# Five of sixteen tiles of a normalised input transposed by DMA, with SyncE's queue in a written order, in a fused attention and SwiGLU gradient kernel

## The chip, the cores and the metric

The kernel runs on one core of a Trainium2 chip. Its engines are TensorE (PE: matmuls, with PEld for its weight loads), VectorE (DVE), ScalarE (ACT), GpSimd (POOL) and SyncE (SP), and 16 DMA engines move data. The metric is the device time of one execution in microseconds; lower is better. The kernel before was timed in three runs.

## The reference

x is 2048 x 640, 32 heads of 20. The kernel returns the block's output and, from grad_out, the gradients of x and of five weights.

```
phi = lambda t: jnp.where(t > 0, t + 1, jnp.exp(t)) + 1e-6
def A(x, wqkv, wo):                      # linear attention
    q, k, v = heads of x @ wqkv
    pq, pk = phi(q), phi(k)
    kv = jnp.einsum("bhsd,bhse->bhde", pk, v)
    z = jnp.einsum("bhsd->bhd", pk)
    num = jnp.einsum("bhqd,bhde->bhqe", pq, kv)
    den = jnp.einsum("bhqd,bhd->bhq", pq, z)[..., None] + 1e-6
    return (num / den) @ wo
def B(x, w_gate, w_up, w_down):          # SwiGLU
    return (silu(x @ w_gate) * (x @ w_up)) @ w_down
h = x + A(layernorm(x), wqkv, wo)
out = h + B(layernorm(h), w_gate, w_up, w_down)
out, vjp = jax.vjp(that, A_x, A_wqkv, A_wo, B_w_gate, B_w_up, B_w_down); grads = vjp(grad_out)
```

## The kernel before, in words

The 2048 rows are 16 tiles of 128 (ST = 16), and D = 640 is five blocks of 128 (DT = 5). The work goes stage by stage: first layer norm with k and q (the k/q stage), the products over all rows for attention (ps_y, ps_z, then small matrices), attention's output with the second layer norm (ps_a), the four groups of SwiGLU columns forward and backward (pg, pu, ps_dw), the gradients back through both layer norms (ps_dhn, ps_dp, ps_dk, ps_dxn), and at the end the output (ps_o) with dW_o and dW_v between its tiles. Small groups of matmuls that need only grad_out and w_down (ps_dm, line 405) are spread over the early stages.

The change touches the first of these. In the k/q stage each tile t passes through these steps, each on its own engine:

- `ln1_stats` (272 to 281): DVE takes mean and variance (lines 277 and 280). `ln_rstd` on GpSimd adds epsilon and raises to −0.5 (lines 139 and 140), which gives rstd1.
- `ln1_xn` (288): DVE writes the normalised tile xn from x, mean and rstd. The first three tiles are only centred, and are normalised again near the stage's end.
- `ln1_tr1` (302) and `copy1` (348): TensorE transposes xn in five matmuls against the identity into PSUM (ps_t), and ACT or DVE copies it to xnT. BY_V lists the tiles that DVE copies.
- `kq_mm` (311): 10 matmuls of 320 columns for k, then 10 for q, each followed on ACT by an exponential (316) and a Relu (317).
- `phi` (321 and 322): DVE joins two tiles of the exponential and the Relu into pk or pqa. After every fourth tile it issues the stores of pk, of pqa and of xnT to scratch in DRAM (326, 328 and 329), which later stages read back.

In iteration t of the loop TensorE runs k of tile t, the transposes of tile t + 1, and q of tile t. DVE runs the statistics of tile t + 3, phi of earlier tiles, and xn of tile t + 2 at the iteration's end. In this stage the orders of TensorE, DVE, ACT and GpSimd are the program's own (a manual schedule). SyncE's was left to the scheduler: after x and the k and q weights (wqk), `load_3` (line 218) puts the rest of x, wv and wo (wvo), wdT (three transposed pieces of w_down) and dh2T (grad_out, transposed by DMA in four parts of 512 rows), all in one row, and the stores stand behind. All these DMAs are issued by SP into one queue.

After the stage, `z_sum` (line 477) sums pk over all rows in matmuls with 32 columns of ones, four partial sums in four groups of 32 PSUM partitions. The sum has to be spread to all partitions in more than bf16's accuracy. Before, ACT and DVE each write one number per row with factors from `sgn`, so that half of the rows hold the rounded sum (high) and the others the remainder (low), and one pass of matmuls with `ones16` (2/H everywhere) adds them (ps_zb, 2 matmuls, at line 109 by the helper `mm_row`). GpSimd makes `hot` and `sgn` at the start (240 to 246). Late in the kernel `dwo` (947 to 953) makes one block of dW_o's rows by two matmuls, with all 128 columns of KV as weights.

Of the kernel before, what the change touches and what calls it, by code (L numbers as in the profile page):

```python
# [20 lines left out]
def kernel(  # L21
# [53 lines left out]
    def wk(name, w=D, pool=0):  # L75
        return wpools[pool].tile([P, w], BF16, name=name, tag="w", padded_shape=[P, D])
# [141 lines left out]
    def load_3():  # L218
        for t0 in range(4, ST, 2):
            yield load_x(nc.sync, t0, t0 + 2)  # L220
        yield nc.sync.dma_start(out=wvo[:, 0:5], in_=A_wqkv[:, 2 * D:3 * D].rearrange("(k p) n -> p k n", p=P))
        for j in range(HG):
            yield nc.sync.dma_start(out=wvo[:, 5 + j, :], in_=A_wo[OH[j]:OH[j] + P, :])
        yield load_wdT(wdT, 0)
        for c in range(4):
            yield nc.sync.dma_start_transpose(out=dh2T[:, :, c * 512:(c + 1) * 512], in_=go_flat[c * 512:(c + 1) * 512, :])
        yield load_wdT(wdT, 1)
        yield load_wdT(wdT3, 3)

    with tc.manual_schedule(engines={EngineType.Pool}):  # L230
        ident = const.tile([P, P], BF16, name="ident")
        make_identity(nc, ident[:])
        nhalf = const.tile([P, 4], FP32, name="nhalf")
        nc.vector.memset(nhalf[:], -0.5)
        ones = const.tile([P, P], BF16, name="ones")
        nc.vector.memset(ones[:], 1.0)
        E = const.tile([P, D], BF16, name="E")
        sgn = const.tile([P, 2], FP32, name="sgn")
        hot = const.tile([P, 8], FP32, name="hot")
        nc.gpsimd.memset(hot[:], 1.0)  # L240
        for sign in (1, -1):
            nc.gpsimd.affine_select(out=hot[:], in_=hot[:], pattern=[[-sign * 16, 8]], compare_op=ALU.is_ge, fill=0.0,
                                    base=0 if sign > 0 else 15, channel_multiplier=sign)
        nc.gpsimd.tensor_tensor(out=hot[:, 0:4], in0=hot[:, 0:4], in1=hot[:, 4:8], op=ALU.add)
        nc.gpsimd.tensor_tensor(out=sgn[:, 1:2], in0=hot[:, 1:2], in1=hot[:, 3:4], op=ALU.add)
        nc.gpsimd.tensor_scalar(out=sgn[:, 0:1], in0=sgn[:, 1:2], scalar1=-2.0, scalar2=1.0, op0=ALU.mult, op1=ALU.add)
    ones16 = const.tile([P, P], BF16, name="ones16")
    nc.vector.memset(ones16[:], 2.0 / H)
    zpad = const.tile([P, 4, 64], BF16, name="zpad")
    nc.vector.memset(zpad[:], 0.0)  # L250
    mask = const.tile([P, 160], BF16, name="mask")
# [8 lines left out]
    def load_wdT(dst, g):  # L260
        o = GM if g == 1 else 0
        return nc.sync.dma_start_transpose(out=dst[:, :, o:o + GW[g]], in_=B_w_down[GO[g]:GO[g] + GW[g], :])
# [6 lines left out]
    pk = big.tile([P, ST, D], BF16, name="pk", tag="B")  # L269
    pqa = big.tile([P, ST, D], BF16, name="pqa", tag="B")  # L270
    NC = 3
    BY_V = (1, 2, 3, 6, 9, 12)

    def ln1_stats(t):
        st6 = small.tile([P, 2, 6], FP32, name="st6", tag="st6")
        for ci, (n0, n1) in enumerate(NCH):
            st = nc.vector.bn_stats(out=st6[:, ci, :], in_=x_tm[t // 8][:, t % 8, n0:n1])
            if t == 0 and ci == 0:
                wait_for(st, load_2())
        nc.vector.bn_aggr(out=mv1[:, t, :], in_=st6[:].rearrange("p a b -> p (a b)"))  # L280
        ln_rstd(mv1[:, t:t + 1, :], rstd1, t, 1)
# [37 lines left out]
    def phi(which, t, n=2):  # L319
        e = (pk, pqa)[which][:, t:t + n, :]  # L320
        nc.vector.tensor_scalar(out=e, in0=e, scalar1=1.0, scalar2=1e-6, op0=ALU.min, op1=ALU.add)
        nc.vector.tensor_tensor(out=e, in0=e, in1=rr[:, 2 * which + t // 2 % 2, t % 2:t % 2 + n, :], op=ALU.add)
        if (t + n) % 4 == 0:
            sl = slice(t + n - 4, t + n)
            if which == 0:
                nc.sync.dma_start(out=scr_pk_v[:, sl, :], in_=pk[:, sl, :])
            else:
                nc.sync.dma_start(out=scr_pq_v[:, sl, :], in_=pqa[:, sl, :])
                nc.sync.dma_start(out=scr_xnT[sl].rearrange("t p k c -> p t k c"), in_=xnT[:, sl])

    PIECES = ((0, 3), (3, DT))

    with tc.manual_schedule(engines={EngineType.PE, EngineType.DVE, EngineType.Activation, EngineType.Pool}):

        ps = mm("ps_warm")

        def warm(n):
            for _ in range(n):
                nc.tensor.matmul(ps[:, 0, :P], lhsT=ident[:], rhs=ident[:], start=True, stop=True)

        def copies(t, eng_copy):
            for sl, src in ln1_tr(t):
                c = eng_copy(out=xnT[:, t, sl], in_=src)
                if t == 0 and sl.start == 0:
                    wait_for(c, load_3())

        def copy1(t):
            (nc.vector.tensor_copy if t in BY_V else nc.scalar.copy)(out=xnT[:, t], in_=ln1_tr1(t))

        warm(37)  # L350
        ln1_stats(0)
        ln1_centre(0, 0, 3 * P)
        ln1_centre(0, 3 * P, D)
        copies(0, nc.scalar.copy)
        warm(8)
        ln1_stats(1)
        ln1_centre(1)
        kq_mm(0, 0, lambda: copies(1, nc.vector.tensor_copy), PIECES)
        ln1_stats(2)
        ln1_centre(2)  # L360
        kq_mm(1, 0, None, PIECES)
        ln1_stats(3)
        kq_mm(0, 1, lambda: copy1(2), PIECES)
        phi(0, 0)
        ln1_xn(3)
        kq_mm(1, 1)
        for t in range(2, ST):
            if t == 2:
                ln1_stats(4)
            if t > 3 and t + 3 < ST:  # L370
                ln1_stats(t + 3)
            kq_mm(t, 0, (lambda: copy1(t + 1)) if t + 1 < ST else None)
            if t == 2:
                ln1_stats(5)
            if t == 3:
                ln1_stats(6)
            if t == ST - 1:
                phi(0, t - 1, 1)
            kq_mm(t, 1)
            if t == 3:  # L380
                phi(1, 0)
            elif t == ST - 1:
                phi(0, t, 1)
                phi(1, t - 3)
                phi(1, t - 1)
            elif t > 3:
                phi(t % 2, t - 2 - t % 2)
            if t + 2 < ST:
                ln1_xn(t + 2)
            if ST - NC - 1 <= t < ST - 1:  # L390
                ln1_xn(t - ST + NC + 1)

# [75 lines left out]
    with tc.manual_schedule(engines={EngineType.PE, EngineType.DVE, EngineType.SP}):  # L470
        yk = strips.tile([P, DT * D + HG * P], BF16, name="yk", tag="S")
        Yt = yk[:, :DT * D].rearrange("p (k n) -> p k n", k=DT)
        KVT = yk[:, DT * D:].rearrange("p (j c) -> p j c", j=HG)
        zs = wk("zs")
        zh = wk("zh")

        def z_sum():
            ps = mm("ps_z")
            for ci, (n0, n1) in enumerate(NCH):
                for t in range(ST):  # L480
                    q = t % 4 * H
                    nc.tensor.matmul(ps[q:q + H, ci, :320], lhsT=ones[:, :H], rhs=pk[:, t, n0:n1],
                                     start=(t < 4), stop=(t >= ST - 4))
            nc.scalar.activation(out=half(zh[:]), in_=row(ps), func=ACT.Copy, scale=sgn[:, 0:1])
            nc.vector.scalar_tensor_tensor(out=half(zs[:]), in0=row(ps), scalar=sgn[:, 1:2], in1=half(zh[:]),
                                           op0=ALU.mult, op1=ALU.add)
            nc.vector.memset(KVT, 0.0)

        for i in range(DT):
            ps = mm("ps_y")  # L490
            for ci, (n0, n1) in enumerate(NCH):
                for t in range(ST):
                    nc.tensor.matmul(ps[:, ci, :320], lhsT=xn[:, t, i * P:(i + 1) * P], rhs=pk[:, t, n0:n1],  # L493
                                     start=(t == 0), stop=(t == ST - 1))
                if (i, ci) == (0, 0):
                    z_sum()
            nc.scalar.copy(out=half(Yt[:, i, :]), in_=row(ps))
            if i == 0:
                ps_z = mm("ps_zb")
                mm_row(ps_z, lambda k: ones16[:], lambda k, n0, n1: zs[:, n0:n1], 1)  # L500
                nc.scalar.copy(out=half(zb[:]), in_=row(ps_z))
                masks()
            if 0 < i < 4:
                dm(1)
# [288 lines left out]
    with tc.manual_schedule(engines={EngineType.SP, EngineType.DVE}):  # L793
# [152 lines left out]
        def dwo(j):  # L946
            h0, h1 = HC[j]
            ev = wk("dwo", pool=j % 2)
            ps = mm("ps_dwo")
            for ci, (n0, n1) in enumerate(NCH):  # L950
                nc.tensor.matmul(ps[:, ci, :320], lhsT=KV[:, j, :], rhs=G[:, j, n0:n1], start=True, stop=True)
            nc.scalar.copy(out=half(ev[:]), in_=row(ps))
            nc.gpsimd.dma_start(out=out_3[OH[j] + h0:OH[j] + h1, :], in_=ev[h0:h1, :])

        def dwv(i):
            ev = wk("dwv", pool=1)
# [101 lines left out]
```

## Time and profile before

| | |
|---|---|
| median of 3 runs (lowest to highest) | 817.11 us (817.04 to 817.66) |
| the profiled execution | 817.11 us, of which the span from first to last instruction is 815.4 us |
| granted clock of TensorE | 1.00 |
| k/q matmuls | 320, from 6.5 us to 54.4 us |
| transposes of one tile at line 302 | 70 matmuls (14 tiles), from 10.4 us to 50.4 us |
| SP's queue over 0 to 70 us | 93.4% of the 16 DMA engines' time |
| DMAs out of the stage | 12 stores of 640 KB, issued from 39.7 to 58.0 us |

"Busy" is the time in which an engine has an instruction running. TensorE's matmuls overlap, so the distance from one's start to the next's is what a matmul costs, not its length. In a line of the timeline the first number is the start and the second the length of a run of like instructions, both in microseconds; then come engine, line, operation, tile written and tiles read, shape and count, and in brackets the idle time before it with what ended it. "SPq" is the sequencer that issues DMAs: its length is that of issuing. "Landing" is the time from the start of issue until all data has arrived.

### The profile page before, as it was taken

The page shows a single profiled execution, that of the slowest core. Times are in us where ns is not written, and L with a number is a line of the kernel's source. Part 1 is how long each engine was busy: PE and PEld are TensorE (multiplying, and loading weights), DVE is VectorE, ACT ScalarE, POOL GpSimd, SP SyncE. Part 2 cuts the span into 40 slices and gives each one's busy share as a digit, 9 for nine tenths or more (in the row PEclk, how much of TensorE's full clock was granted, in tenths as well). Part 3 has the DMA queues.
Part 4 walks back from the last instruction along what each step waited for, and adds up shares of the span by engine and source line. Part 5 has one row for each costly group of instructions (what it writes and reads, how often), then busy time and mean ns, then how long its engine had stood idle before and what let it go on. Part 6 is the DMA issues. An engine that isn't in the chain of part 4 may idle for free.

```text
span 815.4 us, 13981 instructions
## 1 busy us (share of the span) xinstructions
PE 810.0 (99%) x5538; PEld 520.2 (64%) x5538; DVE 442.6 (54%) x849; ACT 288.9 (35%) x406; POOL 193.1 (24%) x356
## 2 busy tenths in 40 slices
PE   8999999999999999999999999999999999999998
PEld 6776666555555555555566677777777777777676
DVE  7878787890086028800760147787892366631212
ACT  6982432660184026400831122322312133322010
POOL 4420022222512412221126401211220121112330
PEclk9999999999999999999999999999999999999999
DMA  9994789899769986994498747977499989999952
GB/s 302 193 360 88 171 185 291 184 254 190 201 142 205 224 196 150 213 231 116 117 255 178 276 94 221 217 202 175 113 241 176 170 157 182 169 200 254 250 158 79
DMA packets 278320, 158.61 MB, mean 195 GB/s; under 512 B 235052, under 2 KB 264877, under 8 KB 278256
## 3 DMA queue, kind: packets, MB, share of 16 engines
q1 hardware_dynamic: 251696, 82.12, 54.0%
q0 software_dynamic: 17744, 64.45, 25.5%
q10 hardware_dynamic: 8816, 11.16, 4.4%
q8 instruction: 43, 0.70, 0.4%
q14 instruction: 21, 0.17, 0.1%
HBM read 47.68 MB, written 53.66 MB: 124 GB/s over the span
## 4 chain that ended last, share of the span: by engine, by line
PE 97%; DMA 1%; DVE 1%; ACT 0%; issue 0%; SPq 0%; DVEq 0%; ACTq 0%
PE ps_dw L676 21%; PE ps_dhn L109 14%; PE ps_dxn L928 8%; PE ps_o L990 7%; PE pu L609 7%; PE pg L604 7%; PE ps_kq L311 5%; PE ps_dwqk L109 5%; PE ps_dm L405 5%; PE ps_y L493 3%; PE ps_dp L109 3%; PE ps_gt L735 3%; PE ps_dk L109 3%; PE ps_a L550 2%; PE pdm L405 2%; DMA xr<-in_A_x_dram 1%
## 5 line engine op out<-in xcount | busy, mean ns | idle before, releaser
L109 PE MATMUL ps_dhn<-wgT,cols 128*128 128x320 bf16 x864 | 119.5, 299 | 0.0
L676 PE MATMUL ps_dw<-dd,hn 128*128 128x448 bf16 (+1 forms) x640 | 118.8, 346 | 0.0
L109 PEld LDWEIGHTS <-cols 128*128 128x128 bf16 x864 | 84.4, 98 | 33.0
L676 PEld LDWEIGHTS <-hn 128*128 128x128 bf16 x640 | 62.5, 98 | 54.3
L678 DVE CAST dwev<-ps_dw 128x896 bf16<-128x896 f32 (+3 forms) x12 | 10.9, 908 | 127.3 <-PE ps_dw L676 109.6
L641 POOL DMA_DIRECT2D scr_dT<-stg x64 | 34.6, 541 | 166.6 <-DMA stg<-dd 165.6
L678 ACT CAST dwev<-ps_dw 128x896 bf16<-128x896 f32 (+1 forms) x20 | 17.6, 878 | 157.6 <-PE ps_dw L676 150.6
L147 DVE CUSTOM_DVE_ANT_0 lb_a<-lb_dy,hn 128x640 bf16<-128x640 bf16 x32 | 26.4, 825 | 76.0 <-ACT lb_dy L145 76.0
L609 PE MATMUL pu<-wgu,hnT 128*128 128x448 bf16 (+1 forms) x320 | 63.6, 346 | 0.0
L604 PE MATMUL pg<-wgu,hnT 128*128 128x448 bf16 (+1 forms) x320 | 63.6, 346 | 0.0
L990 PE MATMUL ps_o<-wd,mT 128*128 128x320 bf16 (+3 forms) x462 | 61.1, 295 | 0.0
L676 PE MATMUL ps_dw<-m_s,dh 128*128 128x448 bf16 (+1 forms) x320 | 60.4, 346 | 0.0
L928 PEld LDWEIGHTS <-ring 128*128 128x128 bf16 x480 | 46.9, 98 | 18.3
L990 PEld LDWEIGHTS <-mT 128*128 128x128 bf16 (+1 forms) x462 | 41.7, 97 | 17.5 <-issue 2.6
L928 PE MATMUL ps_dxn<-wqkvT,ring 128*128 128x320 bf16 x320 | 51.3, 299 | 0.0
L676 PEld LDWEIGHTS <-dh 128*128 128x128 bf16 x320 | 31.3, 98 | 27.1
L609 PEld LDWEIGHTS <-hnT 128*128 128x128 bf16 x320 | 31.3, 98 | 27.1
L604 PEld LDWEIGHTS <-hnT 128*128 128x128 bf16 x320 | 31.2, 98 | 27.1
L405 PE MATMUL ps_dm<-wdT,dh2T 128*128 128x448 bf16 (+1 forms) x240 | 47.0, 344 | 0.1
L405 PEld LDWEIGHTS <-dh2T 128*128 128x128 bf16 x320 | 31.0, 98 | 25.1 <-issue 0.3
L311 PE MATMUL ps_kq<-wqk,xnT 128*128 128x320 bf16 x320 | 46.3, 299 | 0.2
L145 ACT ACTIVATE lb_dy<-ps_dhn,rstd 128x640 bf16<-128x640 f32 x16 | 12.7, 793 | 88.6 <-PE ps_dhn L109 88.6
(171 smaller groups left out, 1274.7 us busy)
## 6 DMA issues: line engine op xcount, KB each, us to landing
scr_dT<-stg POOLq DMA_DIRECT2D x48, 224.0 KB, 3.6
cols<-scr_dT POOLq DMA_DIRECT2D x6, 1728.0 KB, 8.5
scr_m<-m_s POOLq DMA_DIRECT2D x12, 448.0 KB, 4.6
cols<-scr_dT ACTq DMA_DIRECT2D x2, 1728.0 KB, 8.8
out_dram<-dwev POOLq DMA_DIRECT2D x30, 112.0 KB, 3.3
scr_dT<-stg POOLq DMA_DIRECT2D x16, 192.0 KB, 2.4
scr_pk<-pk SPq DMA_DIRECT2D x4, 640.0 KB, 8.4
scr_xnT<-xnT SPq DMA_DIRECT2D x4, 640.0 KB, 8.5
```

The costliest lines, as they stand in the source:

```text
L109: nc.tensor.matmul(ps[:, ci, :320], lhsT=lhs(k), rhs=rhs(k, *NCH[ci]), start=(start and k == 0), stop=(stop and k == n - 1))
L147: nc.vector.tensor_tensor_reduce(out=a[:], in0=dy[:], in1=xhat, scale=1.0, scalar=0.0, op0=ALU.mult, op1=ALU.add, accum_out=sums[:, 1:2])
L311: nc.tensor.matmul(ps[:, ci, :320], lhsT=xnT[:, t, k, :], rhs=wqk[:, k, w0 + n0:w0 + n1], start=(k == 0), stop=(k == DT - 1))
L405: nc.tensor.matmul(ps[:, c, :w], lhsT=dh2T[:, kt, (t + c) * P:(t + c + 1) * P], rhs=wdT[:, kt, o:o + w], start=(kt == 0), stop=(kt == DT - 1))
L493: nc.tensor.matmul(ps[:, ci, :320], lhsT=xn[:, t, i * P:(i + 1) * P], rhs=pk[:, t, n0:n1], start=(t == 0), stop=(t == ST - 1))
L604: nc.tensor.matmul(pg[:, c, :w], lhsT=hnT[:, kt, (t + c) * P:(t + c + 1) * P], rhs=wg[:, kt, 0:w], start=(kt == 0), stop=(kt == DT - 1))
L609: nc.tensor.matmul(pu[:, c, :w], lhsT=hnT[:, kt, (t + c) * P:(t + c + 1) * P], rhs=wg[:, kt, w:2 * w], start=(kt == 0), stop=(kt == DT - 1))
L641: nc.gpsimd.dma_start(out=scr_dT[t + c, :, KO[g]:KO[g] + GK[g], :], in_=stg[:, :GK[g], :])
L676: nc.tensor.matmul(ps[:, c, :w], lhsT=lhs(t), rhs=rhs(t), start=(t == 0), stop=(t == ST - 1))
L678: last = copy(out=ev[:, :len(parts), :w], in_=ps[:, :len(parts), :w])
L928: nc.tensor.matmul(ps[:, ci, :320], lhsT=lhs[:, i, :], rhs=rhs[:, i, n0:n1], start=(k == 0 and i == 0), stop=(k == 2 and i == DT - 1))
L990: nc.tensor.matmul(po(t, ci), lhsT=mTs[t // 4][r, t % 4, j, :], rhs=wd[r, j, n0:n1], start=(t, ci) not in opened, stop=last)
```

## The change

The loads of dh2T's last two parts, of wv and of wo move out of `load_3` into functions of their own, and so do the stores out of `phi`. A table `after` says behind which iteration of the loop each is issued; SyncE joins the manual schedule, so that its DMAs stand in the program's order, and each waits there for its data. From tile XD = 11 on, xn is written one step earlier, at the start of iteration t for tile t + 2, and a DMA transpose issued right then writes xnT from it; TensorE's transposes and the PSUM copies of these five tiles go. Tile 12 leaves BY_V for that reason. The z broadcast uses two rounded parts in two tiles, high and low, hence four matmuls in place of two, and `hot` and `sgn` with their GpSimd instructions go. `dwo` computes only the 120 or 40 rows that are stored.

```
     def load_3():
         for t0 in range(4, ST, 2):
             yield load_x(nc.sync, t0, t0 + 2)
-        yield nc.sync.dma_start(out=wvo[:, 0:5], in_=A_wqkv[:, 2 * D:3 * D]...)
-        for j in range(HG):
-            yield nc.sync.dma_start(out=wvo[:, 5 + j, :], in_=A_wo[OH[j]:OH[j] + P, :])
         yield load_wdT(wdT, 0)
-        for c in range(4):
-            yield nc.sync.dma_start_transpose(out=dh2T[:, :, c * 512:(c + 1) * 512], in_=go_flat[c * 512:(c + 1) * 512, :])
-        yield load_wdT(wdT, 1)
-        yield load_wdT(wdT3, 3)
+        yield load_dh2T(0)
+        yield load_dh2T(1)
...
-    BY_V = (1, 2, 3, 6, 9, 12)
+    XD = 11
+    BY_V = (1, 2, 3, 6, 9)
...
+    after = {5: [(store_q, 0), (store_x, 0)], 6: [(load_dh2T, 2)], 7: [(load_dh2T, 3)], 8: [(load_wv,)], 9: [(store_q, 1)],
+             10: [(store_x, 1)], 11: [(load_wo, 0, 2)], 12: [(load_wo, 2, 4)], 13: [(load_wo, 4, 6), (store_q, 2), (store_x, 2)],
+             14: [(store_x, 3), (store_k, 0), (store_k, 1)],
+             15: [(store_k, 2), (load_wdT, wdT, 1), (store_q, 3), (store_k, 3), (load_wdT, wdT3, 3)]}
...
-    with tc.manual_schedule(engines={EngineType.PE, EngineType.DVE, EngineType.Activation, EngineType.Pool}):
+    with tc.manual_schedule(engines={EngineType.PE, EngineType.DVE, EngineType.Activation, EngineType.Pool, EngineType.SP}):
...
         for t in range(2, ST):
             if t == 2:
                 ln1_stats(4)
+            if XD <= t + 2 < ST:
+                ln1_xn(t + 2)
+                nc.sync.dma_start_transpose(out=xnT[:, t + 2], in_=xn[:, t + 2, :])
             if t > 3 and t + 3 < ST:
                 ln1_stats(t + 3)
-            kq_mm(t, 0, (lambda: copy1(t + 1)) if t + 1 < ST else None)
+            kq_mm(t, 0, (lambda: copy1(t + 1)) if t + 1 < XD else None)
...
-            if t + 2 < ST:
+            if t + 2 < XD:
                 ln1_xn(t + 2)
             if ST - NC - 1 <= t < ST - 1:
                 ln1_xn(t - ST + NC + 1)
+            for f, *a in after.get(t, ()):
+                f(*a)
...
-            nc.scalar.activation(out=half(zh[:]), in_=row(ps), func=ACT.Copy, scale=sgn[:, 0:1])
-            nc.vector.scalar_tensor_tensor(out=half(zs[:]), in0=row(ps), scalar=sgn[:, 1:2], in1=half(zh[:]),
-                                           op0=ALU.mult, op1=ALU.add)
+            nc.scalar.copy(out=half(zs[0][:]), in_=row(ps))
+            nc.vector.tensor_tensor(out=half(zs[1][:]), in0=row(ps), in1=half(zs[0][:]), op=ALU.subtract)
...
-                mm_row(ps_z, lambda k: ones16[:], lambda k, n0, n1: zs[:, n0:n1], 1)
+                mm_row(ps_z, lambda k: ones32[:], lambda k, n0, n1: zs[k][:, n0:n1], 2)
...
-                nc.tensor.matmul(ps[:, ci, :320], lhsT=KV[:, j, :], rhs=G[:, j, n0:n1], start=True, stop=True)
-            nc.scalar.copy(out=half(ev[:]), in_=row(ps))
-            nc.gpsimd.dma_start(out=out_3[OH[j] + h0:OH[j] + h1, :], in_=ev[h0:h1, :])
+                nc.tensor.matmul(ps[:h1 - h0, ci, :320], lhsT=KV[:, j, h0:h1], rhs=G[:, j, n0:n1], start=True, stop=True)
+            nc.scalar.copy(out=half(ev[:h1 - h0, :]), in_=ps[:h1 - h0, :, :320])
+            nc.gpsimd.dma_start(out=out_3[OH[j] + h0:OH[j] + h1, :], in_=ev[:h1 - h0, :])
```

More of the change, by code (lines that the diff above doesn't have):

```diff
@@ L220, in load_3, with load_dh2T, load_wv, load_wo @@
             yield load_x(nc.sync, t0, t0 + 2)
-        yield nc.sync.dma_start(out=wvo[:, 0:5], in_=A_wqkv[:, 2 * D:3 * D].rearrange("(k p) n -> p k n", p=P))
-        for j in range(HG):
-            yield nc.sync.dma_start(out=wvo[:, 5 + j, :], in_=A_wo[OH[j]:OH[j] + P, :])
         yield load_wdT(wdT, 0)
-        for c in range(4):
-            yield nc.sync.dma_start_transpose(out=dh2T[:, :, c * 512:(c + 1) * 512], in_=go_flat[c * 512:(c + 1) * 512, :])
-        yield load_wdT(wdT, 1)
-        yield load_wdT(wdT3, 3)
+        yield load_dh2T(0)
+        yield load_dh2T(1)
+    def load_dh2T(c):
+        return nc.sync.dma_start_transpose(out=dh2T[:, :, c * 512:(c + 1) * 512], in_=go_flat[c * 512:(c + 1) * 512, :])
+    def load_wv():
+        nc.sync.dma_start(out=wvo[:, 0:5], in_=A_wqkv[:, 2 * D:3 * D].rearrange("(k p) n -> p k n", p=P))
+    def load_wo(j0, j1):
+        for j in range(j0, j1):
+            nc.sync.dma_start(out=wvo[:, 5 + j, :], in_=A_wo[OH[j]:OH[j] + P, :])
     with tc.manual_schedule(engines={EngineType.Pool}):
@@ L237 @@
         E = const.tile([P, D], BF16, name="E")
[L238 to L248, printed above, removed]
+    ones32 = const.tile([P, P], BF16, name="ones32")
+    nc.vector.memset(ones32[:], 1.0 / H)
     zpad = const.tile([P, 4, 64], BF16, name="zpad")
@@ L322, in phi, with store_k, store_q, store_x @@
         nc.vector.tensor_tensor(out=e, in0=e, in1=rr[:, 2 * which + t // 2 % 2, t % 2:t % 2 + n, :], op=ALU.add)
[L323 to L329, printed above, removed]
+    def store_k(c):
+        nc.sync.dma_start(out=scr_pk_v[:, 4 * c:4 * c + 4, :], in_=pk[:, 4 * c:4 * c + 4, :])
+    def store_q(c):
+        nc.sync.dma_start(out=scr_pq_v[:, 4 * c:4 * c + 4, :], in_=pqa[:, 4 * c:4 * c + 4, :])
+    def store_x(c):
+        nc.sync.dma_start(out=scr_xnT[4 * c:4 * c + 4].rearrange("t p k c -> p t k c"), in_=xnT[:, 4 * c:4 * c + 4])
+    after = {5: [(store_q, 0), (store_x, 0)], 6: [(load_dh2T, 2)], 7: [(load_dh2T, 3)], 8: [(load_wv,)], 9: [(store_q, 1)],
+             10: [(store_x, 1)], 11: [(load_wo, 0, 2)], 12: [(load_wo, 2, 4)], 13: [(load_wo, 4, 6), (store_q, 2), (store_x, 2)],
+             14: [(store_x, 3), (store_k, 0), (store_k, 1)],
+             15: [(store_k, 2), (load_wdT, wdT, 1), (store_q, 3), (store_k, 3), (load_wdT, wdT3, 3)]}
     PIECES = ((0, 3), (3, DT))
-    with tc.manual_schedule(engines={EngineType.PE, EngineType.DVE, EngineType.Activation, EngineType.Pool}):
+    with tc.manual_schedule(engines={EngineType.PE, EngineType.DVE, EngineType.Activation, EngineType.Pool, EngineType.SP}):
         ps = mm("ps_warm")
@@ L473 @@
         KVT = yk[:, DT * D:].rearrange("p (j c) -> p j c", j=HG)
-        zs = wk("zs")
-        zh = wk("zh")
+        zs = [wk("zs"), wk("zl")]
         def z_sum():
```

## The prediction, as it was put on record

> **What bounds the kernel.** I read four views, from the whole to the place of the change. The page's first and fourth parts:
>
> ```profile
> PE 810.0 (99%) x5538; PEld 520.2 (64%) x5538; DVE 442.6 (54%) x849; ACT 288.9 (35%) x406; POOL 193.1 (24%) x356
> ...
> PE 97%; DMA 1%; DVE 1%; ACT 0%; issue 0%; SPq 0%; DVEq 0%; ACTq 0%
> ```
>
> TensorE is busy 99% of the span, and the chain that ended last is 97% TensorE. So an edit is worth the TensorE time that it takes away, less any wait that it brings. The stretches of the k/q stage (11.5 to 52 us) and of what follows it show whether that holds there (busy PE, PEld, DVE, ACT, POOL; granted clock; DMA share; GB/s):
>
> ```profile
> 11.50:35.00 23.50, 23.50 (x194) 17.46 (x194) 20.84 (x50) 22.68 (x36) 9.76 (x17) 1.00 1.11 249
> 35.00:52.00 17.00, 17.00 (x145) 12.71 (x143) 14.73 (x34) 16.25 (x28) 7.48 (x13) 1.00 1.09 311
> 52.00:62.00 10.00, 10.00 (x98) 6.93 (x97) 5.64 (x11) 6.17 (x10) 0.00 (x0) 1.00 1.04 355
> 62.00:97.00 35.00, 35.00 (x270) 22.68 (x269) 26.88 (x20) 12.99 (x17) 0.00 (x0) 1.00 0.61 125
> ```
>
> TensorE is never idle here and its clock is full, but the DMA share is 1.0 or more until 62 us: the queue into which the new transposes go is full. DVE is 87 to 89% busy. The timeline of one iteration, and the z broadcast:
>
> ```profile
> 41.15 0.44 PE L302 MATMUL ps_t<-ident,xn 128*128 128x128 bf16 x5
> 41.43 2.88 PE L311 MATMUL ps_kq<-wqk,xnT 128*128 128x320 bf16 x20
> ...
> 60.14 0.44 PE L109 MATMUL ps_zb<-zs,ones 128*128 128x320 bf16 x2
> 60.41 4.51 PE L493 MATMUL ps_y<-pk,xn 128*128 128x320 bf16 x32
> ```
>
> Starts are what count, since matmuls overlap: five transposes hold TensorE from 41.15 to 41.43, 0.28 us, and the two z matmuls from 60.14 to 60.41, 0.27 us. In the chain of waits 30 k/q matmuls take 4.08 us, so 20 take 2.72; with 0.28 that is the 3.0 us period of an iteration. The queue and DVE:
>
> ```profile
> 24.65 0.82 DVE L322 TENSOR_TENSOR pqa<-pqa,rr 128x1280 bf16<-128x1280 bf16 x1
> ...
> 34.40 0.44 DVE L288 TENSOR_SCALAR xn<-x_tm,mv,rstd 128x640 bf16<-128x640 bf16 x1
> 34.76 0.88 DVE L277 BATCH_NORM_STATS2 st<-x_tm 128x6 f32<-128x320 bf16 x2
> ...
> 35.67 0.21 DVE L280 BATCH_NORM_AGGREGATE mv<-st 128x2 f32<-128x12 f32 x1
> ...
> 36.40 1.19 POOL L140 TENSOR_TENSOR rstd<-lnv,nhalf 128x1 f32<-128x1 f32 x1
> ```
>
> The first row is when q's tiles 2 and 3 are finished, for which SP will wait; the others are DVE's and GpSimd's steps from xn(10) to the rstd of tile 12, whose lengths set how early an xn can go to the queue.
>
> **What goes, and what comes (TensorE).** The transposes of tiles 11 to 15 (at 38.15, 41.15, 44.14, 47.14 and 50.13) go: 5 x 0.28 = −1.40 us. The z broadcast has four matmuls for two: +0.27. Its inputs take as long as before: a plain ACT copy (a 128x640 PSUM cast took 0.70) for a scaled one (0.79), and a DVE subtraction (a 128x640 operation with PSUM took 0.82) for the three-operand one (0.88). In before the second ended at 59.79, 0.2 us ahead of the weight load at 60.01; without that cover a late input would cost its lateness. Net −1.13.
>
> **Edits at nothing.** The GpSimd setup that goes lies at 1.3 to 8.6 us, and TensorE waits there for DVE's xn (5.49). The four ACT copies and the DVE copy (0.69 and 0.49 each) go from engines that TensorE does not wait for. The dW_o matmuls keep 320 moving columns, hence their time. wv and wo are needed from 85 us and land by about 55; wdT's later parts from about 94. DMA drained by about 65 in before; the added transposes (4 us) and a gap of some 3 us move that to about 72, and the pqsT transposes, issued at 70, are first read at 97.6: their cover is 10 us.
>
> **The new wait.** k/q of tile t now waits for a DMA. Without the transposes, TensorE would reach tile 11 at 39.5 (38.15 + 10 matmuls), and then 42.2, 44.95, 47.7 and 50.4. Two chains feed it.
>
> First, DVE and GpSimd. xn(11) now follows xn(10) directly: 34.8 to 35.2. Then each xn needs its rstd: statistics 1.1 us, then GpSimd, whose power at 36.40 lasted 1.19 because it ended 0.4 after DVE's two-operand operation at 36.34 (elsewhere it took 0.57). Per tile: xn 0.4, statistics 1.1, phi 1.3, 0.4 of waiting: 3.2 us against TensorE's 2.72. So xn is ready at 35.2, 38.4, 41.6, 44.9 and 48.1. The pqsT transposes, the same size out of SBUF, landed 2.7 us after issue (median), 1.2 of it issue: 37.9, 41.1, 44.3, 47.6, 50.8. By this chain alone only tile 15 is late, by 0.4.
>
> Second, the queue itself. Landings stood in order of issue and a fixed distance apart: dh2T at 27.8, 31.7, 34.5, 37.7 (3.3 apart, from 2.8 to 3.9), the 640 KB stores from 44.1 to 65.2 (1.9 apart), wv 2.3 behind the last load of x (19.2 after 16.9). SP now holds back the first stores until phi of q's tiles 2 and 3 (25.5, the row at 24.65). Stores of 800 KB into an emptier queue landed 4.4 after issue, so this one of 640 KB at about 29.4. Behind it in order: xnT store 31.3, dh2T 2 at 34.6, dh2T 3 at 37.9, wv 40.2, and xnT of tile 11 (a quarter of a dh2T, 0.8) at 41.0: 1.5 late. With the shortest distances (1.7, 2.8, 2.8, 2.0, 0.7) it is 39.4, on time; with the longest (3.1, 3.9, 3.9, 2.7, 0.9) 43.9, 4.4 late. The next two each have one store ahead (1.9 + 0.8 = 2.7, TensorE's own pace), the last two only 320 KB: once late, the queue brings no further loss. Behind each waiting transpose on SP stand only stores and weights that nobody needs before 64 us.
>
> So the stall is 0.4 (DVE's chain) to 4.4 us. I take 1.0, between the DVE chain's 0.4 and the mean queue's 1.5, because dh2T's spacing of 3.3 is also SP's own time to issue one (3.1), and two smaller transposes at the end of the row (wdT, 448 and 384 rows) landed 2.8 and 1.9 apart, 3.2 and 2.5 per 512 rows: the DMA engines alone may be quicker than the mean.
>
> [...] The trace has SBUF transposes of five 128x128 blocks landing in 2.7 us. [...] Here 640 KB of dh2T took 3.3 us where a store of 640 KB took 1.9. [...]
>
> **Sum.** The profiled execution took 817.11 us, of which 815.4 span; it equals the median of the runs shown. 817.11 − 1.40 + 0.27 + 1.0 = 817.0.
>
> **Rivals.**
> - Forecast (0.42): the first DMA transpose arrives about 1 us late (0.6 to 1.6 of stall), and most of the saving is given back: 816.6 to 817.6.
> - On time (0.30): the queue is quicker than its mean; the stall is 0 to 0.6, and the time 817.11 − 1.13 to + 0.6 = 816.0 to 816.6. For it: the shortest distances. Against it: DMA share above 1.0.
> - Late queue (0.25): the place is SP's queue between 25.5 us and tile 11; two stores, two dh2T and wv stand ahead of the first transpose. Its price is the lateness of tile 11 with what the following tiles add; it makes the kernel slower from a stall of 1.13, and measurably (0.2%, 1.6 us) from 2.8. At the longest distances it gives 817.11 − 1.13 + 4.4 = 820.4.
> - The change does more than it says (0.03): DVE and ACT, relieved of copies, let TensorE gain elsewhere; nothing supports it, since TensorE has no idle time to win in the stage. Below 815.5.
>
> About 0.2% (1.63 us) is what a measurement of this kernel can tell from no change. Even on time the gain is 1.13, so faster gets the last rival and a share of error in my sums, 0.04. Slower needs a stall over 2.8: 0.14, of the late queue's 0.25. Same 0.82. The range runs from on time, 815.9, to a stall of 3, 819.0.
>
> **What would show it.** In the profile after: ps_t x45 instead of x70 at the one-tile line; a wait of TensorE (or its weight load) at tile 11's k/q, near 39.5 us, released by the DMA into xnT, of about 1 us, and small ones at 12 to 15; the first xnT transpose landing near 40.5. ps_zb x4 with 0.55 us. The z sum at 56.75 in before would begin near 56.4. If xnT 11 lands before 39.5, the second rival holds; if tiles 12 and 13 stall too, my claim that the queue keeps pace is wrong. I am wrong altogether if another place shows a TensorE wait, at ps_dm (64 us, for dh2T) or ps_a (97 us, for pqsT).

## The result, and the profile after

| | before | after |
|---|---|---|
| median (lowest to highest, 6 runs each) | 817.08 us (816.69 to 817.66) | 819.77 us (818.77 to 820.23) |
| ratio, 95% interval | | 1.0031 (1.0018 to 1.0044) |
| the profiled execution, its span | 817.11 us, 815.4 us | 820.23 us, 818.3 us |
| granted clock over the span | 1.00 | 0.997 |

The change costs 2.7 us, a little more than the range allowed (819.0). The six runs of after fall into two groups, which the explanation needs: three have a mean clock of 1.000 (818.77, 818.99, 819.53) and three one of 0.997 or 0.998 (820.01, 820.14, 820.23). The profile is one of the second group.

The page of after, its first part and the chain that ended last:

```profile
PE 811.3 (99%) x5515; PEld 521.0 (64%) x5515; DVE 442.2 (54%) x848; ACT 287.3 (35%) x402; POOL 193.3 (24%) x350
...
PE 97%; DMA 2%; DVE 1%; SPq 0%; issue 0%; DVEq 0%
```

TensorE has 23 instructions fewer (25 transposes less, two z matmuls more) and is busy 1.3 us longer: busy time rose while work fell, so some of the work ran slower. DMA's share of the chain went from 1 to 2%. The stretches of the stage (columns as before: busy PE, PEld, DVE, ACT, POOL; granted clock; DMA share; GB/s) show where:

```profile
11.50:35.00 23.50, 23.50 (x195) 17.47 (x194) 20.82 (x50) 22.63 (x36) 10.19 (x17) 1.00 0.98 220
35.00:52.00 17.00, 14.71 (x100) 9.92 (x99) 13.34 (x30) 12.31 (x20) 8.32 (x13) 0.90 1.05 258
```

The second row is the one that changed in kind. Between 35 and 52 us TensorE is idle for 2.29 us, and the clock granted in that stretch is 0.90. The timeline of TensorE from there:

```profile
42.01 15.43 PE L308 MATMUL ps_kq<-wqk,xnT 128*128 128x320 bf16 x100 [2.29 <-DMA xnT<-xn]
57.28 2.34 PE L500 MATMUL ps_y<-pk,xn 128*128 128x320 bf16 x16
...
62.93 0.30 PE L109 MATMUL ps_zb<-zs,ones 128*128 128x320 bf16 x1
...
63.34 0.30 PE L109 MATMUL ps_zb<-zl,ones 128*128 128x320 bf16 x1
63.48 0.71 PE L500 MATMUL ps_y<-pk,xn 128*128 128x320 bf16 x4
```

The 100 matmuls are tiles 11 to 15, and one wait stands ahead of them. By starts, the last matmul of tile 10 is at 39.42 and the first of tile 11 at 42.01; less one matmul's 0.14 that is a stall of 2.45 us. No later tile waits. But tile 11 took 4.40 us (42.01 to 46.41), and tiles 12 to 15 took 2.72 each. The small stretches around it give the reason:

```profile
39.00:42.00 3.00, 0.72 (x6) 0.29 (x3) 2.40 (x6) 2.16 (x4) 1.54 (x2) 1.00 1.12 328
42.00:43.00 1.00, 0.99 (x6) 0.65 (x7) 0.97 (x4) 0.00 (x0) 0.17 (x1) 0.72 1.04 382
43.00:44.00 1.00, 1.00 (x5) 0.55 (x4) 0.90 (x2) 0.00 (x0) 0.92 (x2) 0.50 1.20 341
...
45.00:46.00 1.00, 1.00 (x6) 0.55 (x4) 0.97 (x4) 0.81 (x2) 0.00 (x0) 0.57 1.24 282
46.00:47.00 1.00, 1.00 (x10) 0.73 (x8) 0.90 (x2) 0.39 (x1) 0.86 (x2) 1.00 0.75 211
```

After the idle time the clock falls to 0.5, at 42.444, and stays there for 3.413 us; TensorE is "busy" all along, with 5 matmuls in a microsecond where it has 10 afterwards. That costs 3.413 / 2 = 1.7 us and is no idle time at all, so a list of waits doesn't show it. Why tile 11 was late, SP's queue tells:

```profile
25.55 0.38 SPq L325 DMA_DIRECT2D scr_pq<-pqa  x1
25.98 0.65 SPq L328 DMA_DIRECT2D scr_xnT<-xnT  x1
26.67 9.09 SPq L226 DMA_TRANSPOSE dh2T<-in_grad_out_dram  x2
35.80 0.58 SPq L229 DMA_DIRECT2D wvo<-in_A_wqkv_dram  x1
36.48 1.21 SPq L376 DMA_TRANSPOSE xnT<-xn  x1
```

Two dh2T transposes took SP 9.09 us to issue behind the two stores: the first 5.8, where one took 3.1 to 3.6 in before. So SP reached tile 11's transpose at 36.48, while DVE had written that tile at 35.25. It landed at 41.97, 5.5 after its issue, behind dh2T's last part (37.8) and wv (41.42). The answers on the single issues give the microseconds from issue to landing, in order from 25.55 on (read with the starts above; the second dh2T was issued at 32.50):

```profile
scr_pq<-pqa SPq DMA_DIRECT2D x1, 640.0 KB, 5.0
scr_xnT<-xnT SPq DMA_DIRECT2D x1, 640.0 KB, 6.1
dh2T<-in_grad_out_dram SPq DMA_TRANSPOSE x1, 8.6
dh2T<-in_grad_out_dram SPq DMA_TRANSPOSE x1, 5.3
wvo<-in_A_wqkv_dram SPq DMA_DIRECT2D x1, 800.0 KB, 5.6
xnT<-xn SPq DMA_TRANSPOSE x1, 5.5
```

So tile 11 landed 0.55 us behind wv, and wv 3.6 behind dh2T's last part.

**The account of the profiled execution.** Transposes −1.38, z broadcast +0.27, stall +2.45, half clock +1.7: +3.0, against +2.9 of span (818.3 − 815.4). Up to the first ps_y matmul (54.49 before, 57.28 after) it is +2.8, pg stands 2.76 later (146.02, 148.78) and the last matmul 2.98 (812.09, 815.07): nearly all of it happens in the stage.

### The profile page after: what moved, and what is told of

Same layout as the page of the kernel before. It is cut to its first block, busy times and chain, and to the rows that moved or that the text cites. A ratio compares the mean times of both kernels' runs of the same rounds, so it can differ in the third digit from the quotient of the medians.

```text
span 818.3 us, 13931 instructions
## 1 busy us (share of the span) xinstructions
PE 811.3 (99%) x5515; PEld 521.0 (64%) x5515; DVE 442.2 (54%) x848; ACT 287.3 (35%) x402; POOL 193.3 (24%) x350
## 4 chain that ended last, share of the span: by engine, by line
PE 97%; DMA 2%; DVE 1%; SPq 0%; issue 0%; DVEq 0%
PE ps_dw L683 21%; PE ps_dhn L109 14%; PE ps_dxn L935 8%; PE ps_o L997 7%; PE pg L611 7%; PE pu L616 7%; PE ps_dwqk L109 5%; PE ps_dm L414 5%; PE ps_kq L308 4%; PE ps_y L500 3%; PE ps_gt L742 3%; PE ps_a L557 3%; PE ps_dk L109 3%; PE ps_dp L109 3%; PE pdm L414 2%; DMA xnT<-xn 1%
## 5 line engine op out<-in xcount | busy, mean ns | idle before, releaser
L648 POOL DMA_DIRECT2D scr_dT<-stg x64 | 34.6, 541 | 160.2 <-DMA stg<-dd 160.0
L616 PEld LDWEIGHTS <-hnT 128*128 128x128 bf16 x320 | 31.3, 98 | 27.1
L683 PEld LDWEIGHTS <-dh 128*128 128x128 bf16 x320 | 31.3, 98 | 27.1
L611 PEld LDWEIGHTS <-hnT 128*128 128x128 bf16 x320 | 31.3, 98 | 27.0
```

The costliest lines, as they stand in the source:

```text
L611: nc.tensor.matmul(pg[:, c, :w], lhsT=hnT[:, kt, (t + c) * P:(t + c + 1) * P], rhs=wg[:, kt, 0:w], start=(kt == 0), stop=(kt == DT - 1))
L616: nc.tensor.matmul(pu[:, c, :w], lhsT=hnT[:, kt, (t + c) * P:(t + c + 1) * P], rhs=wg[:, kt, w:2 * w], start=(kt == 0), stop=(kt == DT - 1))
L648: nc.gpsimd.dma_start(out=scr_dT[t + c, :, KO[g]:KO[g] + GK[g], :], in_=stg[:, :GK[g], :])
L683: nc.tensor.matmul(ps[:, c, :w], lhsT=lhs(t), rhs=rhs(t), start=(t == 0), stop=(t == ST - 1))
```

## The experiments

Theory at the start: the late queue, one wait at tile 11 from what SP has ahead of the first transpose, and the half clock that follows from the idle time. Rivals: that SP's written order, or the z broadcast and the small edits, cost time by themselves; that DVE's chain is too slow for transposes by DMA in any order. "Control" is the kernel before, timed beside each experiment.

### e1: wv behind the first transposes

```
-  8: [(load_wv,)], 11: [(load_wo, 0, 2)], 12: [(load_wo, 2, 4)]
+  11: [(load_wv,)], 12: [(load_wo, 0, 4)]
```

> The changed kernel with wv's load moved from iteration 8 to iteration 11 of the loop and wo's first part from 11 to 12, so that 800 KB less stands ahead of the transposes of tiles 11 and 12. If the wait at tile 11 comes from what is queued ahead of its transpose (theory), wv's 2.0 us between two landings (39.4 to 41.4 in the changed kernel) go, tile 11 lands near 40.0 in place of 42.0, TensorE waits 0.4 us in place of 2.5 and keeps its clock: about 817.1, 2.0 under the changed kernel's undisturbed runs and 3.0 under those that lost the clock. If it comes from xn's own lateness or from the transposes' own latency (rival), the landing stays near 42 and the time near 819.8.

Measured: 818.40 us (817.47 to 821.65, 12 runs), control 816.99, ratio 1.0024 (1.0013 to 1.0035); the theory had said 817.1. Its 39.4 for dh2T's last part in the changed kernel is a misreading, the median of two issues taken for one: that part landed at 37.8, so wv's share was 3.6 us and not 2.0. Without wv ahead of it tile 11 landed at 38.9, 2.6 after its issue (36.23) and 0.6 behind dh2T's last part, and didn't wait: the stall of after was wv's place. But TensorE's timeline has two new waits, at tile 13 (the row names ACT, but that tile's transpose landed at 46.22) and at tile 14, and SP's rows show what stood ahead of the second:

```profile
46.27 2.89 PE L308 MATMUL ps_kq<-wqk,xnT 128*128 128x320 bf16 x20 [0.77 <-ACT pqa L313]
51.44 7.28 PE L308 MATMUL ps_kq<-wqk,xnT 128*128 128x320 bf16 x40 [2.28 <-DMA xnT<-xn]
```

```profile
43.35 0.58 SPq L229 DMA_DIRECT2D wvo<-in_A_wqkv_dram  x1
45.30 1.20 SPq L376 DMA_TRANSPOSE xnT<-xn  x1
```

Tile 14's transpose (45.30) is now behind wv, which landed at 50.70, and the stall of 2.45 us has moved from tile 11 to tile 14, with a half clock again (0.5 from 51.465 for 3.413 us). Tile 15's (48.76), behind four loads of wo, came in time. The load was relocated, not removed. Four of the twelve runs are at 820.38 to 821.65 and the others at 817.47 to 818.74. Of the four, one has a mean clock of 0.998, one of 0.999 (which single runs of the control have too) and two of 1.000, so the half clock alone doesn't explain that group.

### e2: nothing ahead of the transposes that can wait

```
     def load_3(): ...
-        yield load_dh2T(0); yield load_dh2T(1)
+        for c in range(4): yield load_dh2T(c)
+        yield load_wv()
-    after = {5: [(store_q, 0), (store_x, 0)], 6: [(load_dh2T, 2)], 7: [(load_dh2T, 3)], 8: [(load_wv,)], ...
+    after = {9: [(store_q, 0)], 10: [(store_x, 0)], 11: [(store_q, 1)], 12: [(store_x, 1)], 13: [(load_wo, 0, 4)], ...
```

> The changed kernel with all four parts of dh2T and wv issued right behind x, before the loop, and one 640 KB store behind each of the transposes of tiles 11 to 14 (the stores wait longer). Theory: the queue is empty when tile 11 is issued at 35.3; it lands 2.7 to 3.0 us later, before 39.5; the later ones are held by the DVE and GpSimd chain (xn ready every 3.2 us), which makes tile 15 late by 0.4 us or so: 817.1 - 1.38 + 0.27 + 0.4 = 816.4. Rival (a DMA transpose with stores beside it always takes over 5 us): stall near 1 to 2 us again, 817.5 or more.

Measured: 816.88 us (816.48 to 818.19, 11 runs), control 816.99, ratio 0.9999 (0.9990 to 1.0007). All runs have a clock of 1.000. (The theory had said 816.4.) With the same transposes and the same matmuls, and only other places for them in SP's queue, the whole loss is gone: the late queue is shown. SP's rows for the first three transposes, and TensorE:

```profile
35.13 1.20 SPq L376 DMA_TRANSPOSE xnT<-xn  x1
...
38.37 1.20 SPq L376 DMA_TRANSPOSE xnT<-xn  x1
...
41.60 1.29 SPq L376 DMA_TRANSPOSE xnT<-xn  x1
```

```profile
45.61 8.49 PE L309 MATMUL ps_kq<-wqk,xnT 128*128 128x320 bf16 x60 [0.58 <-DMA xnT<-xn]
53.93 2.34 PE L500 MATMUL ps_y<-pk,xn 128*128 128x320 bf16 x16
```

SP now waits for DVE: the issues are 3.23 us apart, the pace of DVE's and GpSimd's chain. One stall is left, at tile 13 (0.75 us, its transpose landed at 45.56, 4.0 after issue), and 0.16 at tile 14. ps_y begins at 53.93, 0.56 earlier than in before.

### e3 and e4: the order alone, the z broadcast alone

e3 is after with `XD = 16` and tile 12 back in BY_V: all transposes are TensorE's, the rest is the change. e4 is before with only the two z parts (`zs`, `zl`, `ones32`, four matmuls).

> The changed kernel with all tiles transposed on TensorE as before (XD = 16, tile 12 copied by DVE again) but SP's queue in its written order and the four z matmuls. Theory: the loss is all in the DMA transposes of the five tiles, so that only the z broadcast's 0.27 us remains: 817.4. Rival (the written order of SP, with the later weights behind the stores, costs by itself somewhere after the stage): 818 or more.

> The kernel before with the change's z broadcast alone (four matmuls over high and low parts; the GpSimd setup of the sign columns goes), all else as before. Theory: two more matmuls on the path, +0.27 us, 817.3. Rival (the shorter setup and the simpler ACT and DVE steps pay for it, or the extra wait for the low part costs more): 817.0 or less, or over 817.6.

Measured: e3 817.50 us (817.06 to 818.82, 11 runs), control 816.99, ratio 1.0004 (0.9996 to 1.0013); e4 817.56 us (817.02 to 823.44, 11 runs), control 817.11, ratio 1.0010 (0.9996 to 1.0024). Neither interval excludes no change. Against their controls they are +0.51 and +0.45, 0.06 us apart. e3 has the written order of SP's queue and the smaller `dwo` beyond what e4 has, so those edits cost nothing that can be seen; the intervals reach some 0.7 and 1.1 us to either side. What the two share is the z broadcast, for which 0.27 was expected.

### e5 and e8: the stall without idle time

Ahead of tile 11's k in the kernel after, 16 (e5) or 8 (e8) matmuls that nothing reads, into a PSUM tile of their own:

```
+            if t == XD:
+                pf = mm("ps_fill")
+                for _ in range(16):
+                    nc.tensor.matmul(pf[:, 0, :320], lhsT=ident[:], rhs=wqk[:, 0, 0:320], start=True, stop=True)
```

> The changed kernel with 16 matmuls of 320 columns (some 2.2 us), whose result nobody reads, put on TensorE where it waits for tile 11. They lie inside the wait, so by themselves they cost next to nothing. Theory (two terms: a wait of 2.5 us, and a window of 3.41 us at half clock behind it in some of the runs, 1.7 us): the clock stays at 1.000 in every run and the median comes to that of the changed kernel's runs without the loss, 818.9, with no run above 819.6. Rival (the half clock isn't set by that wait, or the spread of the changed kernel's runs has another source): the runs still lie in two groups, 818.9 and 820.1, some at 0.997.

> The changed kernel with 8 unread matmuls (1.1 us) in TensorE's wait for tile 11 in place of 16, which leaves about 1.4 us of it idle. Theory (what loses the clock is the length of the idle time, 2.5 us with none, none lost with 0.3 left): with 1.4 us idle the clock holds too, 818.9 in all runs. Rival (any idle of over a microsecond can lose it): some runs near 820.1 at a clock of 0.997 again.

Measured: e5 818.99 us (818.74 to 820.41, 9 runs), control 816.99, ratio 1.0025 (1.0016 to 1.0035); e8 819.41 us (818.90 to 820.11, 9 runs), control 817.11, ratio 1.0027 (1.0017 to 1.0037). The stretch of e5, then of e8:

```profile
35.00:52.00 17.00, 16.79 (x127) 11.76 (x125) 14.45 (x32) 13.61 (x23) 8.33 (x13) 1.00 1.06 256
```

```profile
35.00:52.00 17.00, 15.46 (x117) 10.77 (x115) 14.47 (x33) 13.43 (x22) 8.33 (x13) 1.00 1.07 257
```

Tile 11 starts as late as in after (41.94 and 42.26), but the clock stays 1.00. None of the 18 runs has a clock below 0.999, where three of after's six had 0.997 or 0.998. So the half clock in this place comes from TensorE's idle time: 2.45 us of it was enough in half of six runs, about 1.4 us (e8) in none of nine. (A low clock isn't confined to this wait: one run of e4, whose profile has no such wait, took 823.44 us at 0.996.) It is also seen what it is worth: e5's median equals that of after's three undisturbed runs, 818.99, and the other three lie 1.15 us higher (820.14). The larger part of the loss, some 2 us, remains without it: it is the stall, less what the transposes save. e8 lies 0.5 over its forecast of 818.9 although its clock held; in its profile tile 11 starts 0.3 later than in e5, and tile 13 waits 0.5 where it waits 0.25 in e5.

### e6 and e7: the best order with before's z, and DVE's statistics taken ahead

e6 is e2 with the z broadcast of before. e7 is e6 with the statistics of tiles 12 to 15 taken an iteration or more earlier, and xn of tile 10 ahead of phi, so that SP gets its tiles sooner:

```
-            if t > 3 and t + 3 < ST:
-                ln1_stats(t + 3)
+            if t > 3 and t + 3 + (t >= 9) < ST:
+                ln1_stats(t + 3 + (t >= 9))
...
+                if t == 8:
+                    ln1_xn(10)
...
+            if t == 7:
+                ln1_stats(12)
```

> The kernel with dh2T and wv early and the stores behind (the second experiment, 816.88) with the z broadcast of before. Theory: that experiment's time less the two matmuls, 0.27 us: 816.6, 0.4 under before, of the saving of 1.38 some 1.0 lost to waits at tiles 13 to 15, whose xn comes every 3.2 us. Rival (the z edit costs nothing): 816.9.

> The kernel e6_best with the statistics of tile 12 taken in iteration 7, from then on one tile further ahead, and xn of tile 10 ahead of phi in iteration 8, so that no xn waits for GpSimd's rstd. Theory (the remaining waits come from the chain statistics, GpSimd's power, xn): xn comes every 2.8 us in place of 3.2, tile 15 is ready at 46.4 in place of 48.1, no wait is left, and the whole saving of 1.38 us shows: 815.7. Rival (the waits that are left are the queue's, from the store ahead of each transpose): 816.6, as e6_best.

Measured: e6 817.11 us (816.62 to 818.91, 11 runs), control 817.11, ratio 0.9995 (0.9985 to 1.0006); e7 816.99 us (816.50 to 818.02, 11 runs), same control, ratio 0.9998 (0.9990 to 1.0007). The theories had said 816.6 and 815.7, and neither gain came. In e7 the transposes are issued 2.7 to 2.8 us apart for the most part (35.53, 38.21, 40.89, 43.58, 46.64), yet tile 13 still waits 0.9 us and tile 15 0.4. That DVE's chain was the limit behind e2's stall is refuted: issued sooner (40.89 for 41.60 in e2), tile 13 lands no sooner (45.70 for 45.56). The store ahead of it isn't enough to explain that, since tile 12 has one too and landed 2.6 us after its issue in e2. The last two numbers of e2's rows, DMA share and GB/s, show a pause while tile 13 is under way:

```profile
41.50:42.50 1.00, 1.00 (x9) 0.73 (x8) 0.96 (x4) 0.94 (x3) 0.00 (x0) 1.00 1.06 358
43.50:44.50 1.00, 1.00 (x10) 0.72 (x8) 0.54 (x2) 0.94 (x3) 0.82 (x1) 1.00 0.21 6
```

In e6, e7 and e11b the same microsecond moved 5, 25 and 8 GB/s. What causes the pause, and whether the store has a part in it, wasn't tested. The waits of TensorE (total, times, longest, in us) also show a place of which the prediction says nothing; first e6, then e7:

```profile
PE ps_dw L694 <- DMA dh<-in_grad_out_dram: 1.3, 1, 1.3
```

```profile
PE ps_dw L698 <- DMA dh<-in_grad_out_dram: 0.8, 1, 0.8
```

An earlier TensorE meets a load of grad_out (`dh2`, by GpSimd) that didn't get earlier. In e6 GpSimd issues its fourth part at 169.94 (167.2 in before), because a store queued ahead of it had waited for its data, and it lands at 179.15 (176.22 in before):

```profile
168.76 1.18 POOL L659 DMA_DIRECT2D scr_dT<-stg  x2 [13.98 <-DMA stg<-dd]
169.94 0.76 POOL L602 DMA_DIRECT2D dh<-in_grad_out_dram  x1
```

Both profiles are of executions about 1 us above their kernel's median (818.19 for 817.11, 818.02 for 816.99). So this wait may belong to those executions; that the median run has it isn't shown.

### e10b and e11b: those loads earlier

The loads of `dh2` are issued at t == 0 of the first SwiGLU group instead of t == 2: in e10b in the kernel before, in e11b in e6.

> The kernel before with the same earlier loads of dh2 and nothing else changed. In its profile TensorE doesn't wait there, so theory and rival both expect 817.1; a gain here would mean that the wait strikes some runs of the kernel before too, and would be no part of the change.

> The kernel e6_best (the statistics in their old order) with the earlier loads of dh2. Theory: 816.2, of the saving of 1.38 us some 0.5 to 0.8 lost to tiles 13 to 15. Against e9b_dh2_first it shows again what the statistics taken further ahead are worth in the stage: 0.2 to 0.5 us less in e9b if tiles 13 to 15 wait for DVE's chain, nothing if they wait for the queue.

Measured: e10b 817.80 us (817.27 to 819.17, 11 runs), control 817.02, ratio 1.0011 (1.0002 to 1.0020); e11b 816.92 us (816.70 to 817.87, 11 runs), same control, ratio 0.9999 (0.9990 to 1.0007). In e11b the wait at ps_dw is gone and the one at tile 13 is left (0.7 us); in e10b, where no change was expected, the same move alone costs 0.8 us. Its profile has no new TensorE wait: its last matmul starts 0.3 us later than in before (812.37 after 812.09), and the output's tail behind it is 0.66 longer. Why, stays open. So e11b's result (816.2 was expected) may be a gain of the transposes beside a cost of the moved loads, and the two can't be told apart further with these runs; against their controls e6 and e11b lie at 0.00 and −0.10. The statistics taken ahead together with the earlier loads, which the last expectation calls e9b, were not measured.

No version is measurably faster than before; e2, e6, e7 and e11b are level with it.

## Why the prediction was wrong, step by step

- **What goes and comes: right.** The five transposes' −1.40 is −1.38 in the profile, and where the queue is clear (e2) ps_y begins 0.56 earlier with 0.91 us of stalls: −1.38 + 0.91 = −0.47, near that. The four z matmuls start 0.55 us ahead of what follows them (62.93 to 63.48) in place of 0.27. e4's +0.45 has a second part that I didn't foresee, outside the span: time less span is 1.91 us on average in e2 and 1.70 in e6, which differ in the z broadcast alone, and 1.90 in e4. It isn't the broadcast's own, though: e1, which differs from after in the table alone, has 2.00 for 1.91.
- **Edits at nothing: not contradicted.** e3 against e4 shows no cost of the order and of `dwo`, within intervals of 0.7 us and more. Neither ps_dm nor ps_a waits in after.
- **The new wait, first chain: right.** The forecast of xn was 35.2, 38.4 and 41.6; DVE's rows of after give the ends 35.25, 38.48 and 41.70, and e2's issues are 3.23 apart for my 3.2.

```profile
34.45 0.80 DVE L285 TENSOR_SCALAR xn<-x_tm,mv,rstd 128x640 bf16<-128x640 bf16 x2
38.03 0.45 DVE L285 TENSOR_SCALAR xn<-x_tm,mv,rstd 128x640 bf16<-128x640 bf16 x1 [0.46 <-POOL rstd L140]
41.26 0.44 DVE L285 TENSOR_SCALAR xn<-x_tm,mv,rstd 128x640 bf16<-128x640 bf16 x1 [0.46 <-POOL rstd L140]
```

- **The new wait, second chain: the step that failed.** The stall was put at 1.0 us and was 2.45. Landings by mean distances were 29.4, 31.3, 34.6, 37.9, 40.2 and 41.0; measured 30.5, 32.1, 35.3, 37.8, 41.4 and 42.0. Two terms were too small. The first store landed 1.1 later: it took 4.95 us from its issue at 25.55 where I took 4.4, and 25.5 + 4.4 is 29.9, not my 29.4, a slip of half a microsecond. And wv landed 3.6 behind dh2T's last part where I took 2.3, measured on wv behind a load of x. Right behind dh2T the DMA engines moved 60 GB/s (37.2 to 38.2 us), from 38.5 to 39.5 us 303; e2, e5, e6, e7, e8 and e11b have wv 3.2 to 3.9 behind dh2T too. Why it starts slowly isn't shown. The four other distances came out 1.5 shorter together. Without the slip my mean queue gives a stall of 2.0 and a time of 818.0. I took 1.0 instead, on the ground that "the DMA engines alone may be quicker than the mean". For dh2T they were, as far as the last part shows (2.5 behind the one before it, for 3.3), but wv took that back. The argument also leaned on 3.1 us as SP's own time of issue. Behind the stores it was 5.8, and tile 11's transpose was handed to the queue 1.2 us after its data was ready. That this delay cost anything by itself isn't shown: in e1 SP issues tile 11 nearly as late (36.23), and TensorE doesn't wait for it.
- **"The next two keep pace": right in after's profile**, 100 matmuls without a wait, but with help: the half clock gave the later tiles 1.7 us more. In e5 and e8, the same order without it, tile 13 waits 0.25 and 0.5 us. In e1 tiles 13 and 14 stall, in e2 and e7 tile 13 most.
- **What the sum didn't have: the clock.** I counted TensorE's work at the clock of before. In the profiled execution the idle time was followed by 3.413 us at half clock, which cost 1.7 us (tile 11's 20 matmuls took 4.40 us, those of tiles 12 to 15 took 2.72 each), and the three runs with the lower clock lie 1.15 us higher by median. So a matmul didn't cost the same once there was a wait. How long a wait has to be for that isn't shown: it was 2.45 us in the profile, three of the six runs of after have a mean clock of 1.000 all the same, and with about 1.4 us left (e8) none of nine is below 0.999.
- **The rivals.** The late queue (0.25) was it, in place and mechanism. At its own price of 2.45 it gives 817.11 − 1.13 + 2.45 = 818.4, inside my range; the clock and 0.2 us outside the span lead to 820.2 in the profiled execution. On time (0.30) needed a queue that e2 has and after hasn't.

The first group of after, 818.99 against 817.08, is +1.9; the terms without the clock (−1.38 + 0.27 + 2.45 + 0.2) give +1.5. The 0.4 that is left isn't explained; parts may be a wait at tile 13 as in e5 (0.25), and the start of the kernel, which differs between executions (below).

## What to carry to other kernels

A transfer that takes over work from a busy engine is worth what its place in the queue allows: list what stands ahead of it from the last point at which the queue is known, take the mean of the distances and not the hopeful end, and take each distance from a transfer that stood behind one of the same kind (wv landed 2.3 us behind a plain load, 3.6 behind a DMA transpose). Price a new wait of TensorE above its length, since 2.45 us of idle time was followed here by 3.413 us at half clock, 1.7 us more, that no list of waits shows. And when a stage gets shorter, look at what later stages load: a load that doesn't get earlier can become the next wait (ps_dw in the profiles of e6 and e7).

## What the runs showed of the hardware

- The granted clock fell to 0.5 for 3.413 us after 2.45 us without a matmul, in the profiles of after (42.444 to 45.857) and e1 (from 51.465); with 8 matmuls put in, and about 1.4 us idle, it stayed 1.00 (e8, 35 to 52 us). In after that fall comes 37.547 us, 11 times 3.413, behind the first rise to 1.00, and the fall behind the last matmul (at 817.27) 812.37 us, 238 times 3.413, behind it. What decides between the runs of after with a lower mean clock and those without isn't shown.
- The clock first rises to 1.00 at 4.14 us in before and at 4.90 in after; the starts of ps_warm's matmuls are 0.107 us apart up to there and 0.056 behind it. A stage, too, can start at another time in another execution: ps_a's first matmul starts at 97.7 us in before and at 98.3 in e10b, whose one edit takes effect behind it. That is why differences of 0.6 us and less aren't read from a pair of profiles alone.
- A DMA transpose of a tile of five blocks out of SBUF landed 2.6 us after its issue at the shortest (tile 11 in e1, tiles 11 and 12 in e2), 0.6 to 1.0 us behind the transfer ahead of it, and 3.0 to 5.7 in after's queue.
- Issuing a 512-row transpose took SP 3.1 to 3.6 us in before, and 5.8 in after directly behind two stores of 640 KB. It also took 4.5 once in e2, behind other transposes alone.
- Time less span differs from program to program and in one program's runs stays within some 0.06 us of its mean: 1.71 us in before, 1.91 in after, 2.00 in e1. What lies there the trace doesn't show.
- In e2, e6, e7 and e11b it is tile 13 that is late; from 43.5 to 44.5 us the DMA engines moved 5 to 25 GB/s, from 41.5 to 42.5 us 341 to 358. What causes the pause isn't shown.
